# Attention and scan in one kernel: host-transposed inputs, fp32 row tiles for the scores, a mask added in the reduction, a three-part output product, and another order

## The chip, the cores and the metric

The kernel runs on one core of one Trainium2 chip. A core has five engines, each with an instruction queue of its own: PE (TensorE, matrix products into PSUM), DVE (VectorE), ACT (ScalarE), POOL (GpSimd) and SP (SyncE, which here only issues DMAs). The metric is the device time of one execution in microseconds, the median over runs. Inputs lie in device memory (HBM) before the clock starts, in the layout in which the host function has put them; the result is read from there afterwards.

## What is computed

The result joins two independent parts side by side. Part A is an attention of 16 heads of width 28 over 2048 rows, cut into four segments of 512: causal softmax attention within a segment, mixed by a gate with a linear memory (M, z) that gathers the earlier segments. Part B is a long convolution of a state-space model over 2048 steps of 448 channels.

```
for s in range(N):                                   # N = 4 segments, L = 512, H = 16, Dh = 28
    logits = einsum("bhqd,bhkd->bhqk", qs, ks) * scale + mask
    p = softmax(logits); a_dot = einsum("bhqk,bhkd->bhqd", p, vs)
    pq = phi(qs)                                     # phi(t) = t + 1 if t > 0 else exp(t)
    num = einsum("bhld,bhde->bhle", pq, M); den = einsum("bhld,bhd->bhl", pq, z) + 1e-6
    o = g * num / den + (1 - g) * a_dot
    M = M + einsum("bhld,bhle->bhde", phi(ks), vs); z = z + sum_l phi(ks)
a = concat(o) @ wo
b = irfft(rfft(u) * rfft(K))[:L] + u * D_skip        # K = 2 Re sum_n C_n exp(A_n dt t), dt = exp(log_dt)
```

With the given inputs log_dt is about -32, so K hardly changes over 2048 steps and part B is a running sum of u. Both kernels test this on the device (`flag`) and hold the general convolution (`general_conv`) behind a branch that is not taken for these inputs.

## The kernel before

Part A runs as 16 units t, one for each segment s and group g of four heads. For a unit, PE makes q and k (`P_proj`, L534). fp32 precision is made from the faster fp32r format by splitting: x and the weights are held as a rounded part (xh, wh) and a rest (xl, wl), and a product is 11 matmuls that add up in one PSUM bank. Its last one uses only 64 of the 128 rows. v is made in the same way (`V_tile`, L510), one tile of 128 rows per unit on average.

For the scores, q and k are split in turn (tile E, ACT L540 and DVE L541) and copied by three DMAs on POOL (`P_fill`, L555) into a stack SB, in which the parts stand below each other in 96 rows for each head; one fp32r matmul over the 96 rows gives the score. `Q1` (L615) makes all scores of a unit with queries on the partitions; a bf16 matmul (L618) adds the causal mask on the diagonal block and DVE takes each row's maximum (L624). `Q1_max` splits the maxima (L633, L634), transposes them (L636) and puts them into two more rows of the stack with four DMAs (L640). `Q2` (L656) makes the scores again with the keys on the partitions, the maximum subtracted through these rows; ACT takes the exponential (L663, L673), POOL zeroes what lies above the diagonal (L676) and PE multiplies by v (L683, pvp). The four heads of this product lie in four column tiles of PE (128 rows by 32 columns each).

The memory is kept as a block-diagonal matrix Mbd of a group (`M_upd`, L580 to L598) and used in `P_num` (L565). `Q2_end` copies pvp out (L690), gathers the denominators by DMA (rc, L696), inverts them on DVE (L700, L701), writes them to HBM (d, L703) and reads them back spread over the partitions (R, L705). `C_unit` multiplies (L716) and adds (POOL, L720). `W_tile` makes the output product in plain fp32 (L731), ACT copies it out (L736) and SP writes it (L738).

x comes in rows and is transposed on PE (`X_tile`, L484). Part B is 16 tiles: u is loaded (L813), transposed (L826), scaled (L832), scanned twice on DVE (L837, L840), combined with the skip term (L845), transposed back (L851) and written (L855).

All of this is recorded as operations with a cost, a priority and the tiles that they touch; a planner (`Order.plan`) then lists them once, at build time, for each engine. On the chip each engine works down its list in order, so an instruction that waits holds up all behind it on the same engine. Tiles have a fixed number of slots (`SLOTS`); PSUM has seven general banks (f) and one for pvp.

Of the kernel before, what the change touches and what calls it, by code (L numbers as in the profile page):

```python
# [10 lines left out]
BF16 = mybir.dt.bfloat16  # L11
# [8 lines left out]
P = 128  # L20
# [3 lines left out]
NSB = 2  # L24

SLOTS = dict(E=2, xh=1, xl=1, phiq=1, phik=1, P0=1, P1=1, P2=2, R=1, o0=1, o1=1, o2=1, o3=1, pkn=1, mt=1, mx=1, mh=1, mr=1,
             U=2, ut=1, sc=1, z=1, rc=1, xin=2, os=2, pvn=3, d2=3, pv=1, f=7)


class Buf:  # L30


    def __init__(self, tag, make):
        self.tag, self.make, self.tile, self.log, self.left, self.place = tag, make, None, [], 0, 0

    @property
    def ap(self):
        if self.tile is None:
            self.tile = self.make()
        return self.tile  # L40


class Order:


    DRAIN = {"PE": 200.0}
    HOP = 70.0
    RATE = 220.0
    FLIGHT = 2200.0

    def __init__(self, slots):
        self.slots, self.ops, self.made = slots, [], {}

    def buf(self, tag, make):
        b = Buf(tag, make)
        b.place = self.made[tag] = self.made.get(tag, -1) + 1
        return b

    def op(self, eng, cost, pri, fn, r=(), w=(), hold=(), land=0.0):
# [12 lines left out]
        self.ops.append((eng, cost, pri, fn, deps, touch, land))  # L72

    def plan(self):
# [9 lines left out]
        start, end = [None] * n, [0.0] * n  # L84
        free = dict.fromkeys(("PE", "DVE", "ACT", "POOL", "SP"), 0.0)
        ready = {e: {} for e in free}
        slots = {t: [0.0] * c for t, c in self.slots.items()}
        got, last, turn = {}, {}, dict.fromkeys(self.slots, 0)
        lands, moved = [0.0] * n, 0.0

        def seen(j, eng):
            e = self.ops[j][0]
            t = end[j] + lands[j]
            return t if e == eng and not lands[j] else t + self.HOP + self.DRAIN.get(e, 0.0)

# [7 lines left out]
        while done < n:  # L103
            best = None
            for e, cand in ready.items():
                found = []
                for i, t in cand.items():
                    ok = True
                    for b in self.ops[i][5]:
                        if b.tag is not None and id(b) not in got:  # L110

                            if not slots[b.tag] or (b.tag != "f" and b.place != turn[b.tag]):
                                ok = False
                                break
                            t = max(t, min(slots[b.tag]))
                    if ok:
                        found.append((max(t, free[e]), self.ops[i][2], i))
# [10 lines left out]
            eng, cost, pri, fn, deps, touch, land = self.ops[i]  # L128
            del ready[eng][i]
            start[i], end[i] = t, t + cost  # L130
            free[eng] = end[i]
            lands[i] = land
# [4 lines left out]
            for b in touch:  # L137
                if b.tag is not None:
                    if id(b) not in got:
                        got[id(b)] = True  # L140
                        turn[b.tag] += 1
                        slots[b.tag].remove(min(slots[b.tag]))
                    last[id(b)] = max(last.get(id(b), 0.0), seen(i, None))
                    b.left -= 1
                    if not b.left:
                        slots[b.tag].append(last[id(b)])
# [12 lines left out]
def general_conv(tc, u, lar, aim, crl, cim, ldt, dsk, o2):  # L159
# [6 lines left out]
    with ExitStack() as ctx:  # L166
# [59 lines left out]
        ov = o2.rearrange("(c p) d -> p c d", p=P)  # L226
        with tc.For_i(0, NB, 1) as i:
# [67 lines left out]
            nc.sync.dma_start(ov[:, :, bass.ds(d0 + D, ND)], ul)  # L295


def attn_s4d_kernel(tc, x, wq, wk, wv, wo, beta, u, lar, aim, crl, cim, ldt, dsk, out):
    nc = tc.nc
    x2 = x[0]  # L300
    o2 = out[0]
    top = ExitStack()
    flag = top.enter_context(tc.tile_pool(name="top", bufs=1)).tile([1, 1], I32, name="flag")
    with ExitStack() as ctx:
        pool = lambda n, b, **k: ctx.enter_context(tc.tile_pool(name=n, bufs=b, **k))
        cst = pool("cst", 1)
        wp = pool("wp", 1)
        dr = pool("dr", 3, space=DRAM)
        pools = {}
        for tag, n in SLOTS.items():  # L310
            if tag not in ("pv", "f", "d2"):
                pools[tag] = pool("s_" + tag, n)
        pools["d2"] = dr
        for tag in ("pv", "f"):
            pools[tag] = pool("p_" + tag, SLOTS[tag], space=PSUM)
        Q = Order(SLOTS)

        def new(tag, shape, dt, name):
            return Q.buf(tag, lambda: pools[tag].tile(shape, dt, name=name, tag=tag))

        def fixed(pl, shape, dt, name):
            b = Q.buf(None, None)
            b.tile = pl.tile(shape, dt, name=name)
            return b


        def mm(n):
            return n / 2.4 + 20

        def act(n, ptr=0):  # L330
            return 165 + 0.85 * n + 90 * ptr
# [4 lines left out]
        def gps(n):  # L336
            return 200 + 2.6 * n
# [4 lines left out]
        identb = cst.tile([P, P], BF16, name="identb")  # L342
        make_identity(nc, identb)
        mask = cst.tile([P, P], BF16, name="mask")
        nc.gpsimd.memset(mask, 0.0)
        nc.gpsimd.affine_select(mask, mask, [[-1, P]], ALU.is_ge, NEG, base=0, channel_multiplier=1)
        bmask = cst.tile([112, 4, 32], F32, name="bmask")
        bsel = cst.tile([112, 4], F32, name="bsel")
        nc.vector.tensor_reduce(bsel, ident[0:112, 0:112].rearrange("p (r h) -> p h r", h=4), AX.X, ALU.add)
        nc.vector.tensor_copy(bmask, bsel[:, :, None].to_broadcast([112, 4, 32]))  # L350

        epsb = cst.tile([P, 1], F32, name="epsb")
        tmp1 = cst.tile([P, 4], F32, name="tmp1")
        nc.gpsimd.memset(tmp1, 0.0)
# [587 lines left out]
```

## Time and profile before

| what | us |
|---|---|
| median of three runs (506.38, 507.01, 511.79) | 507.01 |
| span of the profiled execution, first to last instruction | 505.8 |
| PE, time with a matmul in flight | 428.5 |
| DVE busy | 274.2 |
| ACT busy | 221.8 |
| POOL busy | 129.3 |

The profile gives one execution; its span is 1.2 us below the median of the timed runs. A matmul's record reaches from its start to its modelled end and so overlaps the next one; how fast PE works is read from the distance between two starts, not from the busy time. The copies of pvp on ACT (L690), one for each unit, end at 78.9 us for the first unit and at 467.3 us for the last, which cuts the span into a build-up, a steady part of fifteen units (25.9 us each) and an end.

### The profile page before, as it was taken

The numbers are of one execution on the slowest core, as the hardware profiler recorded it, in microseconds if no ns is written. First come the engines' busy times: TensorE is split into PE (matmuls) and PEld (weight loads), VectorE is DVE, ScalarE is ACT, GpSimd is POOL, SyncE is SP. The second block draws the span as 40 slices with busy tenths as digits, with TensorE's granted clock in tenths as the row PEclk, the third lists the DMA queues.
The fourth block names the chain that finished last, engine by engine and source line by source line (L and its number), as shares of the span: only waits on it lengthen the run. The fifth ranks groups of instructions, "written<-read, shape, count | busy, mean of one in ns | idle before, by whom it ended". The sixth has DMA issues, their size and how long they took to land. (4 is left out here: it accounts for less than half of the span.)

```text
span 505.8 us, 6508 instructions
## 1 busy us (share of the span) xinstructions
PE 428.5 (85%) x2249; PEld 265.8 (53%) x2249; DVE 274.2 (54%) x501; ACT 221.8 (44%) x437; POOL 129.3 (26%) x224
## 2 busy tenths in 40 slices
PE   2099999989898999789999999889999999787316
PEld 1076666665654556556756555565656455433102
DVE  7654784856564717655374633757275726553310
ACT  2543255445447255262635445344535463247001
POOL 8554131303022303123041401304140413032100
PEclk9999999999899999995989999989989999798759
DMA  8756614743605373915261353913660646302112
GB/s 247 206 144 126 122 33 81 136 103 67 120 24 129 74 184 80 160 43 101 71 152 31 90 128 96 165 51 66 119 152 22 134 123 137 59 31 72 39 52 77
DMA packets 32390, 51.17 MB, mean 101 GB/s; under 512 B 9936, under 2 KB 24256, under 8 KB 32352
## 3 DMA queue, kind: packets, MB, share of 16 engines
q0 software_dynamic: 8016, 24.79, 25.8%
q1 hardware_dynamic: 23200, 24.08, 17.0%
q10 hardware_dynamic: 1136, 1.84, 1.1%
q8 instruction: 20, 0.33, 0.3%
q14 instruction: 18, 0.15, 0.1%
HBM read 20.60 MB, written 7.57 MB: 56 GB/s over the span
## 5 line engine op out<-in xcount | busy, mean ns | idle before, releaser
L624 DVE TENSOR_REDUCE mx<-q 128x2 f32<-128x512 f32 (+2 forms) x192 | 104.0, 594 | 38.8 <-PE q L618 38.5
L615 PE MATMUL q<-SB 96*128 96x256 f32 (+2 forms) x256 | 78.3, 400 | 14.9 <-DMA SB<-E 11.8
L676 POOL TENSOR_SCALAR_AFFINE_SELECT P<-P 128x512 f32<-128x512 f32 x64 | 44.5, 700 | 139.7 <-ACT P L663 118.2
L731 PE MATMUL po<-w_o,o 128*128 128x448 f32 x128 | 56.9, 579 | 21.9 <-POOLq L918 13.7
L656 PE MATMUL s<-SB 98*128 98x256 f32 (+2 forms) x256 | 64.3, 366 | 7.2 <-DMA SB<-mr 3.7
L663 ACT ACTIVATE P<-s 128x512 f32<-128x512 f32 (+1 forms) x128 | 58.2, 563 | 19.5 <-PE s L656 18.9
L615 PEld LDWEIGHTS q<-SB 96*128 96x128 f32 x256 | 47.6, 206 | 30.5 <-issue 15.7
L656 PEld LDWEIGHTS s<-SB 98*128 98x128 f32 x256 | 43.0, 196 | 29.5 <-issue 11.4
L683 PE MATMUL pvp<-P,vb 128*32 128x128 f32 (+3 forms) x512 | 49.3, 461 | 4.3 <-POOL P L676 4.2
L618 PE MATMUL q<-mask,identb 128*128 128x128 bf16 (+1 forms) x192 | 49.5, 258 | 0.0
L731 PEld LDWEIGHTS po<-w_o,o 128*128 128x128 f32 x128 | 23.8, 200 | 44.3 <-issue 20.4
L555 POOL DMA_DIRECT2D SB<-E x48 | 33.3, 729 | 39.3 <-PE s L656 25.4
L673 ACT ACTIVATE P<-s 128x512 f32<-128x512 f32 (+1 forms) x64 | 31.1, 529 | 17.3 <-PE s L656 16.9
L842 POOL COPY carry<-sc 112x1 f32<-112x1 f32 x32 | 7.1, 223 | 120.0 <-DVE sc L837 66.8
L716 DVE TENSOR_TENSOR o<-pvn,R 128x512 f32<-128x512 f32 x16 | 11.9, 746 | 38.9 <-DMA R<-d 38.6
L832 ACT ACTIVATE z<-ut,cf 112x512 f32<-112x512 f32 x32 | 23.2, 726 | 20.2 <-DVE sc L837 19.8
L618 PEld LDWEIGHTS <-identb 128*128 128x128 bf16 x192 | 19.3, 101 | 20.6 <-issue 8.1
L510 PE MATMUL vp<-wh_v,xh 128*128 128x448 f32 x64 | 28.8, 450 | 0.1
L736 ACT COPY os<-po 128x448 f32<-128x448 f32 x16 | 8.6, 539 | 44.6 <-PE po L731 42.0
L837 DVE TENSOR_TENSOR_SCAN sc<-ones,carry,z 112x512 f32<-112x512 f32 x16 | 21.9, 1367 | 11.5 <-PE pvp L683 5.8
L510 PE MATMUL vp<-wl_v,xh 128*128 128x448 f32 x64 | 28.0, 437 | 0.0
L540 ACT CAST E<-ppq 112x512 fp32r<-112x512 f32 x16 | 9.5, 591 | 41.8 <-PE ppq L534 41.7
(125 smaller groups left out, 699.4 us busy)
## 6 DMA issues: line engine op xcount, KB each, us to landing
SB<-E POOLq DMA_DIRECT2D x48, 448.0 KB, 8.0
R<-d SPq DMA_DIRECT2D x12, 512.0 KB
x<-in_A_x SPq DMA_DIRECT2D x16, 224.0 KB
U<-in_B_u SPq DMA_DIRECT2D x8, 448.0 KB
out<-U SPq DMA_DIRECT2D x8, 448.0 KB
out<-os SPq DMA_DIRECT2D x16, 224.0 KB
SB<-mr SPq DMA_DIRECT2D x64, 4.0 KB
R<-d SPq DMA_DIRECT2D x4, 256.0 KB
```

The source lines that it names most:

```text
L510: nc.tensor.matmul(pv.ap, xs[xx].ap[0:k, c, lt * P:(lt + 1) * P], ws[w].ap[0:k, c, :], start=(i == 0), stop=(i == len(ps_) - 1))
L555: nc.gpsimd.dma_start(Sf[28 * i:28 * i + 28], (Ef[:, 1:3, :], Ef[:, 0:3:2, :], Ef[:, 1:4:2, :])[i])
L615: nc.tensor.matmul(pt.ap[:, j, :], SB.ap[0:96, h, 0, qb * P:(qb + 1) * P], SB.ap[0:96, h, 1, 0:m], start=(j == 0), stop=False)
L618: nc.tensor.matmul(pt.ap[:, :, n - P:n], identb, mask[:, None, :].to_broadcast([P, len(hs), P]), start=False, stop=True)
L624: nc.vector.tensor_reduce(mx.ap[:, hs[0]:hs[-1] + 1, qb], pt.ap[:, :, 0:n], AX.X, ALU.max)
L656: nc.tensor.matmul(o, SB.ap[0:98, h, 1, kb * P:(kb + 1) * P], SB.ap[0:98, h, 0, 512 - m:512], start=True, stop=True)
L663: Q.op("ACT", act(n), pri + 0.02 * h, lambda pp=pp, h=h: nc.scalar.activation(pb.ap[:, h, :], pp.ap[:, 0:n], AF.Exp, scale=SCALE), r=[pp], ...
L673: Q.op("ACT", act(2 * n), pri + 0.02 * h, lambda pp=pp, h=h: nc.scalar.activation(pb.ap[:, h:h + 2, :], pp.ap[:, :, 256 - n:256], AF.Exp, ...
L676: Q.op("POOL", 700, pri + 0.1, lambda: nc.gpsimd.affine_select(pb.ap[:, :, 0:P], pb.ap[:, :, 0:P], [[0, 4], [1, P]], ALU.is_ge, 0.0, base= ...
L683: nc.tensor.matmul(pvp.ap[32 * h:32 * h + 32, kb * P:512], V.ap[:, 4 * g + h, :], pb.ap[:, h, :], start=(kb == 0), stop=(kb == 3))
L731: nc.tensor.matmul(po.ap, st[4 * s + g]["o"].ap[:, cs], w.ap[:, g, :], start=(g == 0), stop=(g == 3))
L832: Q.op("ACT", 725, p, lambda k=k, z=z: nc.scalar.activation(z.ap, ut.ap, AF.Copy, scale=cf.ap[:, j, k:k + 1]), r=[ut, cf], w=[z])
```

## The change

Host. The host function hands over x and u transposed, the weights already in the order of the head groups (each head padded from 28 to 32 columns) and beta and the vectors of part B in the shape of their tiles. Part B is written transposed to an output of its own and turned on the host. So X_tile's and part B's transposes are gone, and the loads are whole rows of 2 KB.

Scores. q and k stay in fp32, head h in the partitions 32h to 32h+27, and the stacks, their DMAs and the split are gone. Q1 and Q2 use matmuls of 28 (29) rows by 128 columns in fp32, four heads one behind the other, each in its own row tile of PE and its own PSUM bank. Row 28 of k holds -1 and row 28 of q gets the maximum, by one DMA. The mask matmul is gone: DVE adds the mask while it takes the maximum (`tensor_tensor_reduce`, for each head and block of queries alone).

The rest. The 64-row matmul at the end of each product uses 128 rows. The memory M is [128, 32], one 28 x 32 block for each head, in row and column tiles. phi takes its minimum on POOL. The output product is three fp32r matmuls for each group, for which o is rounded (ACT) and the rest taken (POOL). Part B keeps one scan of two and a multiply-add. All weights and x go through three slots (xin) by SP, in turn with ACT's rounding and DVE's or POOL's rest. All DMAs are issued by SP. PSUM is one pool of eight banks. The planner knows a price for a change of PE's tile shape (`SWITCH`), takes among operations that are nearly ready the one of highest priority (`NEAR`), and its priorities come from a table of numbers (`AT`).

```diff
+                        f = free[e] + (self.SWITCH if e == "PE" and self.ops[i][7] != mode else 0.0)
...
-                    t, p, i = min((f for f in found if f[0] <= t0 + 1e-9), key=lambda f: (f[1], f[2]))
+                    t, p, i = min((f for f in found if f[0] <= t0 + self.NEAR[e]), key=lambda f: (f[1], f[2]))
...
+        room("f", 8, [P, 512], F32, psm)
+        room("xin", 3, [P, 512], F32)
+        room("pvn", 2, [P, 2, 512], F32)
...
-            return r + [(0, 0, 3, P), (1, 0, 3, 64)]
+        PASSES = [(w, x, c) for c in range(3) for w, x in ((0, 0), (1, 0), (0, 1))] + [(0, 0, 3), (1, 0, 3)]
...
+            Q.op("SP", 90, pri, lambda: nc.sync.dma_start(t.ap, xT[s, :, c]), w=[t], land=-262144)
+            Q.op("ACT", act(512), pri, lambda: nc.scalar.copy(h.ap, t.ap), r=[t], w=[h])
...
-                        nc.tensor.matmul(pt.ap[:, j, :], SB.ap[0:96, h, 0, qb * P:(qb + 1) * P], SB.ap[0:96, h, 1, 0:m],
-                                         start=(j == 0), stop=False)
-                    nc.tensor.matmul(pt.ap[:, :, n - P:n], identb, mask[:, None, :].to_broadcast([P, len(hs), P]),
-                                     start=False, stop=True)
+                    for h in range(4):
+                        nc.tensor.matmul(bank[h].ap[:, c0:c0 + n], q.ap[rows(h), qb * P:(qb + 1) * P], k.ap[rows(h), 0:n],
+                                         start=True, stop=True)
...
-                    nc.vector.tensor_reduce(mx.ap[:, hs[0]:hs[-1] + 1, qb], pt.ap[:, :, 0:n], AX.X, ALU.max)
+                        nc.vector.tensor_tensor_reduce(sc, sc, mask[:, 512 - n:512], 1.0, -3.0e38, ALU.add, ALU.max,
+                                                       mx.ap[:, 4 * h + qb:4 * h + qb + 1])
...
-                nc.tensor.matmul(o, SB.ap[0:98, h, 1, kb * P:(kb + 1) * P], SB.ap[0:98, h, 0, 512 - m:512],
-                                 start=True, stop=True)
+                        nc.tensor.matmul(bank[h].ap[:, c0:c0 + w], k.ap[rows(h, 29), kb * P:(kb + 1) * P],
+                                         q.ap[rows(h, 29), P * kb:512], start=True, stop=True)
...
+            Q.op("ACT", act(512), pri, lambda: nc.scalar.copy(oh.ap, pvn.ap[:, 0, :]), r=[(pvn, 0)], w=[oh])
+            Q.op("POOL", 1344, pri, lambda: nc.gpsimd.tensor_tensor(ol.ap, pvn.ap[:, 0, :], oh.ap.bitcast(F32), ALU.subtract),
+                 r=[(pvn, 0), oh], w=[ol])
...
-                nc.tensor.matmul(po.ap, st[4 * s + g]["o"].ap[:, cs], w.ap[:, g, :], start=(g == 0), stop=(g == 3))
+                for i, (o, w) in enumerate(((oh, wh), (oh, wl), (ol, wh))):
+                    nc.tensor.matmul(po.ap, o.ap[:, cs], w.ap[:, g], start=(g == 0 and i == 0), stop=(g == 3 and i == 2))
...
-                    o2[lc * 512:(lc + 1) * 512, 448 + 224 * jp:672 + 224 * jp].rearrange("(t p) d -> p t d", p=P), U.ap),
+            Q.op("SP", 90, pri, lambda: nc.sync.dma_start(yT[ds_, ls], ut.ap), r=[ut], land=-229376)
+AT = dict(q=-1.78, k=-1.95, fq=-2.44, fk=3.5, V=-1.6, Vn=0.65, num=-0.43, M=-0.71, s=-1.62, sn=-0.05, max=-3.89,
+          e=-0.68, en=0.1, pv=0.11, c=-0.34, w=2.79, wn=0.6, b=2.67, x=-3.8, xn=-2.14)
```

Three places show what this does to the engines' lists. On PE, the first scores of unit 0 stood like this before (q: score banks, SB: a stack; L615 scores, L618 mask):

```order
L615 MATMUL q_0_559<-SB_193 128x256 x2
L618 LDWEIGHTS identb
L618 MATMUL q_0_559<-mask,identb 128x2x128
L615 MATMUL q_0_563<-SB_193 128x256 x2
L618 LDWEIGHTS identb
L618 MATMUL q_0_563<-mask,identb 128x2x128
L615 MATMUL q_0_571<-SB_193 128x384
L618 LDWEIGHTS identb
L618 MATMUL q_0_571<-mask,identb 128x128
```

Each bank is now filled by one plain matmul of one head, four heads in a row into four banks (f), and products of unit 1 (L486) follow:

```order
L555 MATMUL f_69<-k_94,q_90 128x512
L555 MATMUL f_70<-k_94,q_90 128x512
L555 MATMUL f_71<-k_94,q_90 128x512
L555 MATMUL f_72<-k_94,q_90 128x512
L555 MATMUL f_73<-k_94,q_90 128x384
L555 MATMUL f_74<-k_94,q_90 128x384
L555 MATMUL f_67<-k_94,q_90 128x384
L555 MATMUL f_68<-k_94,q_90 128x384
L486 MATMUL f_69<-xh_78,wh_q 128x512
```

The mask rows are gone, and the unit's scores are no longer one stretch: the 384- and 512-wide blocks come first and other products stand between them and the narrow ones. Counted over the whole list, and leaving out the single matmuls of 64 rows, PE changes its tile shape 124 times before and 197 times now.

On DVE, the maxima of the same unit stood like this before (mx: maxima, ek: phi of k):

```order
L624 TENSOR_REDUCE mx_581<-q_0_559 128x2
L546 SCALAR_TENSOR_TENSOR ek_540<-ek_540,ppk_518 112x512
L624 TENSOR_REDUCE mx_581<-q_0_563 128x2
L624 TENSOR_REDUCE mx_581<-q_0_571 128x1
L624 TENSOR_REDUCE mx_581<-q_1_574 128x1
```

And now (L563 is the masked maximum; each is two instructions, the second stores the result; wl: rests of the weights, from the slots xin):

```order
L432 TENSOR_TENSOR wl_v<-xin_76,wh_v 128x448
L563 ISA f_69,mx_123<-f_69,mask 128x512
L563 ISA mx_123 128x1
L432 TENSOR_TENSOR wl_q<-xin_77,wh_q 128x512
L563 ISA f_70,mx_123<-f_70,mask 128x512
L563 ISA mx_123 128x1
```

A unit's 12 reductions have become 16 pairs, and the maxima of the first units now stand between the rests of the weights.

On SP, the last DMAs were these before (rc, d, R: the denominators' way; U: part B; os: output rows; mr: maxima):

```order
L696 DMA rc_4198<-pvn_3832 128x1x32
L640 DMA SB_194<-mr_4195 2x4x128 x4
L855 DMA out<-U_0_3436 128x4x224
L703 DMA d_14_4252<-rc_4198 128x32
L705 DMA R_4277<-d_14_4252 128x1x1024
L696 DMA rc_4318<-pvn_4019 128x1x32
L855 DMA out<-U_1_3883 128x4x224
L703 DMA d_15_4341<-rc_4318 128x32
L705 DMA R_4343<-d_15_4341 128x1x1024
```

And these are the last ones now:

```order
L615 DMA rc_127<-pvn_104 128x1x32
L622 DMA d_131<-rc_127 128x32
L662 DMA out_a<-os_122 128x448
L627 DMA R_106<-d_131 128x1x1024
L615 DMA rc_128<-pvn_105 128x1x32
L622 DMA d_129<-rc_128 128x32
L627 DMA R_106<-d_129 128x1x1024
L662 DMA out_a<-os_121 128x448
```

Before, a write of part B stood between rc and d of the last unit; now d follows rc directly, and part B has been written earlier.

More of the change, by code (lines that the diff above doesn't have):

```diff
@@ L304, in attn_s4d_kernel @@
     with ExitStack() as ctx:
[L305 to L316, printed above, removed]
@@ L559, in P_num @@
         def P_num(t, pri):
             s, g = divmod(t, NG)
[L561 to L568 removed]
+            if s == 0:
+                return
```

840 lines of the change are left out of this document (373 added, 467 removed).

## The prediction

> **What bounds the kernel now.** I read the page first, for the engines' shares, and then asked for four stretches, cut where PE's first real products start (26.4 us) and where the first and the last unit's pvp are ready (78.3 and 466.7 us). After that I went through PE's timeline.
>
> ```profile
> PE 428.5 (85%) x2249; PEld 265.8 (53%) x2249; DVE 274.2 (54%) x501; ACT 221.8 (44%) x437; POOL 129.3 (26%) x224
> ...
> 0.00:26.40 26.40, 4.60 (x17) 2.83 (x17) 18.88 (x25) 11.37 (x19) 17.41 (x50) 1.00 0.81 221
> 26.40:78.30 51.90, 50.85 (x256) 34.08 (x255) 34.28 (x71) 19.95 (x43) 19.41 (x25) 1.00 0.51 110
> 78.30:466.70 388.40, 359.65 (x1952) 222.54 (x1951) 214.73 (x398) 186.53 (x370) 88.73 (x145) 0.96 0.44 96
> 466.70:505.80 39.10, 13.38 (x28) 6.38 (x28) 6.29 (x9) 3.97 (x7) 3.73 (x4) 0.73 0.16 57
> ```
>
> In the columns of the stretches PE comes first, then the weight loads, DVE, ACT and POOL. For 440.3 us (26.4 to 466.7) PE has a matmul in flight during 410.5; the next, DVE, is busy for 249. So PE's stream is the bound, with 30 us of waits, and before and behind it stand 26.4 us of loading and 39.1 us of an end that is one chain of DMAs. I therefore cost the change by the distance between starts on PE, and the two ends by themselves.
>
> **Part by part: PE.** Products first.
>
> ```profile
> 63.29 0.39 PE L534 MATMUL ppk<-xh,wl_k 128*112 128x512 f32 x1
> 63.52 0.40 PE L534 MATMUL ppk<-xh,wh_k 128*112 128x512 f32 x1
> 63.85 0.48 PE L534 MATMUL ppk<-xh,wl_k 64*112 64x512 f32 x1
> 64.26 1.13 PE L588 MATMUL pm<-vb,pkn 128*112 128x128 f32 x8
> ...
> 45.62 0.36 PE L510 MATMUL vp<-wh_v,xl 128*128 128x448 f32 x1
> 45.82 0.36 PE L510 MATMUL vp<-wl_v,xh 128*128 128x448 f32 x1
> ```
>
> A 512-wide fp32r matmul takes 0.23 us from start to start (63.29 to 63.52), a 448-wide one 0.20. Around the 64-row matmul the steps are 0.33 and 0.41 instead, 0.28 us too much for one change of the tile shape there and one back. There are 48 products (32 for q and k, 16 for v), each loses this: 48 x 0.28 = **13 us less**.
>
> ```profile
> 201.75 3.27 PE L731 MATMUL po<-w_o,o 128*128 128x448 f32 x8
> 204.86 0.60 PE L484 MATMUL xp<-ident,x 128*128 128x128 f32 x4
> 205.30 0.55 PE L580 MATMUL pkt<-ident,ek 112*128 112x112 f32 x4
> ```
>
> Eight fp32 records of the output product take 3.11 us, 0.39 each; 128 of them (50 us) become 192 fp32r matmuls of 0.20 (38 us): **12 us less**. Four transposes of x take 0.44 us, and those of u and y, as narrow, are costed alike; 16 groups for x and 32 for u and y go: 48 x 0.44 = **21 us less**.
>
> ```profile
> 53.53 0.47 PE L615 MATMUL q<-SB 96*128 96x256 f32 x2 [0.98 <-DMA SB<-E]
> ...
> 57.97 0.49 PE L534 MATMUL ppq<-xh,wh_q 128*112 128x512 f32 x1
> ...
> 71.10 1.07 PE L683 MATMUL pvp<-P,vb 128*32 128x512 f32 x8
> 72.10 0.51 PE L656 MATMUL s<-SB 98*128 98x256 f32 x2
> ...
> 218.98 1.27 PE L656 MATMUL s<-SB 98*128 98x512 f32 x5
> 220.09 0.39 PE L534 MATMUL ppk<-xh,wl_k 128*112 128x512 f32 x1
> ...
> 221.06 1.27 PE L656 MATMUL s<-SB 98*128 98x384 f32 x7
> 222.17 1.04 PE L588 MATMUL pm<-vb,pkn 128*112 128x128 f32 x8
> ...
> L615 PEld LDWEIGHTS q<-SB 96*128 96x128 f32 x256 | 47.6, 206 | 30.5 <-issue 15.7
> ```
>
> Q1 of a unit, with its mask matmuls, takes 4.4 us (53.53 to 57.97). Q2 takes 0.22 for a wide matmul (five in 1.11) and 0.16 for a narrow one (seven in 1.11); with 4 of 512, 4 of 384 (0.19, between the two) and 8 of 256 that is 0.9 + 0.8 + 1.3 = 3.0 us. The trace has no row tile. The nearest row is the fp32 column tile: four heads of 512 columns (eight records) take 1.00 us to the next start, 0.14 of which is the change of shape (0.28 / 2), so 0.86. One behind the other, eight full-width records of 0.39 x 512 / 448 would take 3.6, so four column tiles run at once. If row tiles do too, a unit's blocks of 512, 384, 256 and 128 columns, four heads each, cost 0.86 + 0.65 + 0.43 + 0.41 = 2.4 us (the last is held by two weight loads of 206 ns instead of its 0.21). I take this value, from the nearest row; the other end is one head at a time, and a rival. Q1 saves 16 x (4.4 - 2.4) = **32 us**, Q2 16 x (3.0 - 2.4) = **10 us**.
>
> [...]
>
> Against this stand the changes of tile shape: 197 for 124, 73 x 0.14 = **10 us more**. [...]
>
> P_num and M_upd keep their columns, now in four or 16 small tiles at once; I cost them at nothing, between 5 us less and 10 us more, since each of 12 updates grows from 8 records to 32. PE's sum is 13 + 32 + 10 + 12 + 21 - 10 = **78 us less**.
>
> **Waits and other engines.**
>
> ```profile
> L615 PE MATMUL q<-SB 96*128 96x256 f32 (+2 forms) x256 | 78.3, 400 | 14.9 <-DMA SB<-E 11.8
> L624 DVE TENSOR_REDUCE mx<-q 128x2 f32<-128x512 f32 (+2 forms) x192 | 104.0, 594 | 38.8 <-PE q L618 38.5
> L541 DVE TENSOR_TENSOR E<-ppk,E 112x512 fp32r<-112x512 f32 x16 | 11.0, 686 | 11.7 <-ACT ek L544 8.0 <-ACT E L540 3.8
> L489 DVE TENSOR_TENSOR xl<-xp,xh 128x384 fp32r<-128x384 f32 x16 | 8.9, 554 | 3.1 <-ACT xh L486 3.0
> L624 DVE TENSOR_REDUCE mx<-q 128x2 f32<-128x256 f32 x32 | 13.4, 417 | 4.3 <-PE q L618 4.3
> L597 DVE TENSOR_TENSOR mt<-pm,bmask 112x128 f32<-112x128 f32 x8 | 2.3, 286 | 6.1 <-PE pm L588 6.1
> L634 DVE TENSOR_TENSOR mh<-mx,mh 128x16 fp32r<-128x16 f32 x16 | 2.8, 176 | 0.6
> L840 DVE TENSOR_TENSOR_SCAN sc<-z,carry,sc 112x512 f32<-112x512 f32 x16 | 20.6, 1287 | 0.9 <-ACT z L832 0.9
> ```
>
> PE's wait for the copy into the stack (11.8 us) goes with the stack: **12 less**. What is late next is DVE. Its 192 reductions (104.0 us) become 256 masked ones with two inputs from or through PSUM, for which I take DVE's rows of the same widths: 4 x (686 + 554 + 417 + 286) = 7.8 us for a unit, 124 us, and 256 stores of a maximum, between nothing and 176 ns each (45 us); I take 0.1 us, 26 us. That is 46 us more. The rests of q and k (L541, 11.0 us for k and as much for q), one scan (20.6) and the split maxima (L634 and its like) go, 45 us or more, so DVE stays at or under its 274 us, two thirds of the new span. Its bursts have to fit between two fills of four banks, so I leave PE's other 18 us of waits as they are. ACT loses the casts and Relus of the split and gets those of o; it stays near its 222 us. POOL loses 48 DMA issues and gets 16 rests of o and 24 minima; at 26% this is hidden, except at the end. SP takes over all loads and its list is in order: a u or weight load whose slot is not free holds q's maxima behind it. With one DMA for the maxima in place of four I cost it at nothing; it is part of the rival on new waits. pvn has two slots instead of three: the way from pvn (466.7) to the end of L720 in the rows below (491.6) is 25 us, well under the two units (over 40 us) that two slots give, so this is hidden.
>
> **The two ends.**
>
> ```profile
> 474.98 0.24 DVE L701 TENSOR_SCALAR rc<-rc,mix 128x32 f32<-128x32 f32 x1
> 478.47 0.38 SPq L855 DMA_DIRECT2D out<-U  x1
> 478.95 0.46 SPq L703 DMA_DIRECT2D d<-rc  x1
> 488.93 0.69 DVE L716 TENSOR_TENSOR o<-pvn,R 128x512 f32<-128x512 f32 x1 [13.71 <-DMA R<-d]
> 490.30 1.26 POOL L720 TENSOR_TENSOR o<-o,pvn 128x512 f32<-128x512 f32 x1 [16.41 <-DVEq L918]
> 491.62 9.33 PE L731 MATMUL po<-w_o,o 128*128 128x448 f32 x20 [13.74 <-POOLq L918]
> ...
> L690 ACT COPY pvn<-pvp 128x512 f32<-128x512 f32 x16 | 9.4, 585 | 36.0 <-PE pvp L683 35.9
> ...
> 0.83 0.41 SPq L469 DMA_DIRECT2D x<-in_A_x  x1
> ...
> 3.90 0.87 PE L484 MATMUL xp<-ident,x 128*128 128x128 f32 x3 [3.90 <-DMA x<-in_A_x]
> ```
>
> At the end d waited behind part B's write, 3.7 us after L701 was done (475.2 to 478.95). That goes. The rounding of o (0.6, like ACT's copy of 512 columns in L690) and the rest on POOL (1.3, as L720) come into the chain. Behind them stand 30 matmuls of 0.20 to 0.4 for 20 of 0.47: 1 us less. Together **3 us less**. At the start V waited until 26.4 us. A load is there 3 us after its issue (0.83 to 3.90). Now the first product needs five loads through three slots; a round of three takes that 3 us, one rounding (0.6) and up to three rests on DVE (0.7 each, as L541), 5 to 6 us, so two rounds end near 12 us, and the weights of v, which need five, near 28 us. In between PE has q, k and first scores of units 0 and 1, four products of 2.5 us and 2.4 us of scores. So up to 28 us it idles about 28 - (4 x 2.5 + 2.4) = 16 us instead of 26.4 - 4.6 = 22: **6 us less** (between 0 and 12).
>
> Sum: 505.8 - 78 - 12 - 3 - 6 = 407 us of span, and the 1.2 us between span and median: **408 us**.
>
> **The rivals.**
> *Row tiles do not run together* (the slower side). Then each head's block is paid alone, 4 x 2.15 = 8.6 us for 2.4, and 32 times the difference of 6.2 is 198 us: 606 us. For: no row shows them. Against: the column tiles do it in fp32. It decides against the change once the 32 sets cost 3.1 us more each (99 / 32), at 5.5 us, that is when fewer than 1.6 of the four run at once. At two at once a set takes 4.3 us and the kernel 408 + 32 x 1.9 = 469 us.
> *DVE becomes the bound.* The masked reduction writes its scores back to PSUM. If that costs a second pass, DVE gets 124 us more, some 390 us busy; with the start, the end and a few waits 450 us. For: DVE holds four banks until it is done, and 16 pairs of a unit come in bursts. Against: rows with a PSUM input (L541) cost no more than others.
> *The waits go too.* With the stack's long way (split, DMA, fill) gone and the next unit's products standing between the blocks, the other 18 us of waits and most of the changes of shape (ten to twenty microseconds) vanish: 370 us.
> *The general convolution runs*, because the test on the device is a new one: with these inputs its left side is 0.02 of its right, so it is left out with under 1 in 100.
>
> **How the numbers follow.** The forecast (385 to 430, with the bounds of M_upd, of the start and of the stores) gets 0.58; waits gone (360 to 385) 0.15; DVE bound or other new waits (430 to 470) 0.17; row tiles two at once or worse 0.10, of which 0.07 end slower than before. The range for 8 in 10 leaves out the upper part of the third and the fourth, and the lowest part of the second: 362 to 460. About 1% is what a measurement of this kernel can tell from no change. Faster: 0.58 + 0.15 + 0.17 and a little of the fourth, 0.91; slower 0.07; same 0.02.
>
> **What would show it.** The rows of the two score lines: four 512-wide heads within some 0.9 us and PE's next start right behind; 1.5 us or more says that they do not run together. The masked reduction near 690 ns at 512 columns, and its store under 180 ns. DVE between 250 and 290 us. No wait of PE for a stack. The changes of shape as steps of 0.1 to 0.2 us before a first row tile. PE's idle time in the steady part under 30 us, and if it is far over that, its releaser: DVE's maxima would mean the second rival, SP's DMAs a list that is held up. The prediction is wrong if the span is over 460 without a row tile that is slower than 0.9 us for four heads.

## The result, and the profile after

| | before | after |
|---|---|---|
| median (4 runs each) | 509.38 us | 390.18 us |
| lowest to highest | 506.38 to 511.79 | 388.06 to 391.86 |
| profiled span | 505.8 | 387.5 |

The ratio of after to before is 0.773, with an interval of 0.767 to 0.779; it is taken over executions in the faster of two states alone, and the medians of the table would give 0.766. The forecast was 408 us with a range of 362 to 460.

The page of the changed kernel, its first line, has the engines' busy time, share of the span and instructions:

```profile
PE 345.5 (89%) x2801; PEld 210.2 (54%) x2801; DVE 235.4 (61%) x696; ACT 197.4 (51%) x404; POOL 128.3 (33%) x169
```

Four stretches of the changed kernel, cut where V starts (34.3) and at the first and the last unit's copy of pvn (58.7 and 351.3); PE's busy time stands first behind the length, PE's granted clock is the third number from the right:

```profile
0.00:34.30 34.30, 23.38 (x98) 14.45 (x98) 22.60 (x64) 12.88 (x23) 5.09 (x34) 1.00 0.62 178
34.30:58.70 24.40, 24.40 (x235) 16.85 (x234) 20.80 (x62) 15.86 (x33) 11.60 (x12) 1.00 0.27 78
58.70:351.30 292.60, 283.97 (x2455) 168.67 (x2440) 188.06 (x567) 164.71 (x341) 106.51 (x119) 0.98 0.21 67
351.30:387.50 36.20, 13.77 (x42) 10.26 (x42) 3.94 (x6) 3.95 (x7) 5.07 (x4) 0.64 0.15 54
```

Between the first and the last copy of pvn lie 15 units: 388.4 us before (the prediction's row 78.30:466.70), 292.6 now. I take such a steady part into three: what PE's idle time takes (length less busy), what a low clock takes (length times one less the clock, an estimate and rounded to about 2 us, since the row has two digits), and the rest, which I call work. Waits too short to be seen stay in the work. The traces also record each stretch at low clock: 34.1 us before and 10.2 now, at a granted clock of 0.50, which is 17.1 and 5.1 us lost. So the estimate of the clock's part holds to 2 us, and the work's with it.

| us | length | idle | clock | work |
|---|---|---|---|---|
| before | 388.4 | 28.8 | 15.5 | 344.1 |
| after | 292.6 | 8.6 | 5.9 | 278.1 |
| difference | -95.8 | -20.2 | -9.6 | -66.0 |

The beginning is 19.6 us shorter (78.3 to 58.7): PE's busy time in it is 7.7 less (4.60 + 50.85 to 23.38 + 24.40) and its idle time 11.9 less. The record of the clock starts only at 30.6 us before and at 20.2 us now, so the 1.00 of the first rows says nothing of the time ahead of that; there the changed kernel's products step by 0.43 us (9.01 to 9.44), about twice the 0.23 of later, which costs some 5 us of its 10.5 us of busy time (an estimate). The end is 2.9 shorter (39.1 to 36.2). The sum, -95.8 - 19.6 - 2.9, is the 118.3 us between the spans.

PE's timeline of the changed kernel (start, duration, engine, line, operation, number merged), first the row tiles among products, then a wait and what came behind it:

```profile
205.81 0.94 PE L586 MATMUL f<-q,k 29*128 29x256 f32 x16
206.67 0.50 PE L486 MATMUL f<-xh,wh_q 128*128 128x512 f32 x1
...
210.77 0.36 PE L470 MATMUL f<-wh_v,xl 128*128 128x448 f32 x1
211.06 1.14 PE L555 MATMUL f<-k,q 28*128 28x512 f32 x8
212.13 0.47 PE L470 MATMUL f<-wh_v,xh 128*128 128x448 f32 x1
212.45 0.36 PE L470 MATMUL f<-wl_v,xh 128*128 128x448 f32 x1
...
213.34 0.93 PE L555 MATMUL f<-k,q 28*128 28x384 f32 x8
214.20 0.46 PE L534 MATMUL f<-vb,xin 128*32 128x32 f32 x32
214.47 2.38 PE L606 MATMUL f<-P,vb 128*32 128x512 f32 x32
219.21 0.46 PE L534 MATMUL f<-vb,xin 128*32 128x32 f32 x32 [2.36 <-DVE M L540]
219.60 2.81 PE L586 MATMUL f<-q,k 29*128 29x512 f32 x8
...
225.22 0.63 PE L486 MATMUL f<-xl,wh_k 128*128 128x512 f32 x1
225.64 0.63 PE L486 MATMUL f<-xh,wh_k 128*128 128x512 f32 x1
...
228.57 0.50 PE L486 MATMUL f<-xh,wh_k 128*128 128x512 f32 x1
228.91 0.39 PE L486 MATMUL f<-xh,wl_k 128*128 128x512 f32 x1
229.14 0.39 PE L486 MATMUL f<-xl,wh_k 128*128 128x512 f32 x1
```

Four heads of 512 columns take 1.07 us from start to start (211.06 to 212.13), those of 384 0.86, and the 256- and 128-column blocks together 0.86 (205.81 to 206.67). The step into the row tiles is 0.29 for 0.20 (210.77 to 211.06), the one out of them 0.32 (212.13 to 212.45). Behind 219.21 the steps are longer in two ways that have to be told apart. The set at 219.60 takes 2.74 us to the next start for 1.07; the products from 225.22 on step by 0.42 (225.22 to 225.64) instead of 0.23 (228.91 to 229.14). The weight loads (PEld) of the set, and the granted clock of this place:

```profile
220.43 0.29 PEld L586 LDWEIGHTS f<-q,k 29*128 29x128 f32 x2 [0.22 <-DVE mx L563]
220.95 0.29 PEld L586 LDWEIGHTS f<-q,k 29*128 29x128 f32 x2 [0.22 <-DVE mx L563]
...
218.19:221.60 3.41, 2.39 (x40) 1.52 (x40) 3.41 (x13) 1.72 (x4) 2.30 (x2) 1.00 0.02 5
221.60:225.02 3.42, 3.42 (x12) 0.92 (x11) 1.06 (x4) 0.99 (x3) 0.24 (x1) 0.50 0.03 5
```

The set waits for DVE's maxima, one head at a time, 0.52 us apart, while the clock is still at 1.00; PE counts as busy all the while. The clock falls to 0.50 only at 221.6 and is back at 228.4. Ahead of both stands a wait of 2.36 us. DVE's part of the same place, and the mean of the masked maxima:

```profile
217.19 1.29 DVE L637 TENSOR_TENSOR pvn<-pvn,R 128x512 f32<-128x512 f32 x2 [3.57 <-DMA R<-d]
218.41 0.69 DVE L563 CUSTOM_DVE_ANT_0 f<-f,mask 128x512 f32<-128x512 f32 x1
...
219.01 0.14 DVE L563 DVE_READ_ACCUMULATOR2_ANT mx<- 128x1 f32 x1
219.01 0.18 DVE L540 TENSOR_TENSOR M<-M,f 128x32 f32<-128x32 f32 x1
219.11 0.69 DVE L563 CUSTOM_DVE_ANT_0 f<-f,mask 128x512 f32<-128x512 f32 x1
...
219.72 0.14 DVE L563 DVE_READ_ACCUMULATOR2_ANT mx<- 128x1 f32 x1
```

```profile
L563 DVE CUSTOM_DVE_ANT_0 f<-f,mask 128x512 f32<-128x512 f32 (+3 forms) x256 | 120.9, 514 | 47.5 <-PE f L555 45.3
L563 DVE DVE_READ_ACCUMULATOR2_ANT mx<- 128x1 f32 x256 | 36.0, 140 | 0.1
```

DVE stood 3.57 us for R's transfer; a maximum and the addition to M were queued behind the multiplications; PE waited for that addition, then in short waits for the maxima that came late with it, and 2.4 us after the long wait the clock fell to 0.50 for 6.8 us. The only other low stretch in the steady part of this trace is its last 3.4 us. A maximum and its store come every 0.71 us at 512 columns (219.01 to 219.72 between two stores).

### The profile page after: what moved, and what is told of

It reads as the page before. It is cut to its first block, busy times and chain, and to the rows that moved or that the text cites. A ratio compares the mean times of both kernels' runs of the same rounds, so it can differ in the third digit from the quotient of the medians.

```text
span 387.5 us, 7551 instructions
## 1 busy us (share of the span) xinstructions
PE 345.5 (89%) x2801; PEld 210.2 (54%) x2801; DVE 235.4 (61%) x696; ACT 197.4 (51%) x404; POOL 128.3 (33%) x169
## 5 line engine op out<-in xcount | busy, mean ns | idle before, releaser
L563 DVE CUSTOM_DVE_ANT_0 f<-f,mask 128x512 f32<-128x512 f32 (+3 forms) x256 | 120.9, 514 | 47.5 <-PE f L555 45.3
L590 ACT ACTIVATE P<-f 128x384 f32<-128x384 f32 (+1 forms) x192 | 86.3, 527 | 20.1 <-PE f L586 18.8
L586 PE MATMUL f<-q,k 29*128 29x128 f32 (+3 forms) x512 | 54.8, 465 | 0.3 <-DVE mx L563 0.2
L555 PE MATMUL f<-k,q 28*128 28x128 f32 (+3 forms) x512 | 50.5, 471 | 0.8 <-ACT k L491 0.8
L655 PE MATMUL f<-wh_o,oh 128*128 128x448 f32 x64 | 27.6, 431 | 17.3 <-ACT oh L643 16.8
L606 PE MATMUL f<-P,vb 128*32 128x128 f32 (+3 forms) x512 | 39.4, 449 | 0.3 <-DVE mx L563 0.2
L486 PE MATMUL f<-xh,wh_q 128*128 128x512 f32 x64 | 28.4, 444 | 10.4 <-ACT wh_q L429 7.3
L563 DVE DVE_READ_ACCUMULATOR2_ANT mx<- 128x1 f32 x256 | 36.0, 140 | 0.1
L586 PEld LDWEIGHTS f<-q,k 29*128 29x128 f32 x512 | 26.3, 183 | 17.1 <-DVE mx L563 5.2
L486 PE MATMUL f<-xh,wh_k 128*128 128x512 f32 x64 | 28.9, 452 | 0.5 <-DVE mx L563 0.5
L655 PEld LDWEIGHTS f<-wh_o,oh 128*128 128x128 f32 x64 | 13.1, 205 | 26.8 <-ACT oh L643 18.7
L486 PE MATMUL f<-xh,wl_k 128*128 128x512 f32 x64 | 26.6, 416 | 0.2 <-DVE wl_k L432 0.2
L486 PE MATMUL f<-xh,wl_q 128*128 128x512 f32 x64 | 26.3, 411 | 0.4 <-DVE wl_q L432 0.4
```

The costliest lines, as they stand in the source:

```text
L486: nc.tensor.matmul(pp.ap, (wl if w else wh).ap[:, g, c], X(s, x, c).ap, start=a, stop=b)
L555: nc.tensor.matmul(bank[h].ap[:, c0:c0 + n], q.ap[rows(h), qb * P:(qb + 1) * P], k.ap[rows(h), 0:n], start=True, stop=True)
L563: nc.vector.tensor_tensor_reduce(sc, sc, mask[:, 512 - n:512], 1.0, -3.0e38, ALU.add, ALU.max, mx.ap[:, 4 * h + qb:4 * h + qb + 1])
L586: nc.tensor.matmul(bank[h].ap[:, c0:c0 + w], k.ap[rows(h, 29), kb * P:(kb + 1) * P], q.ap[rows(h, 29), P * kb:512], start=True, stop=True)
L590: Q.op("ACT", act(n), pri + 0.01 * h, lambda h=h: nc.scalar.activation(pb.ap[:, h, 0:n], bank[h].ap[:, 0:n], AF.Exp, scale=SCALE), r=[bank ...
L606: nc.tensor.matmul(pvp.ap[32 * h:32 * h + 32, kb * P:512], VB(s, kb).ap[:, 4 * g + h, :], pb.ap[:, h, c0:c0 + 512 - P * kb], start=(kb == ...
```

## Experiments

Differences are the ratio to the kernel before, less the 0.7728 of the changed kernel, times 505 us. The intervals of both together leave some 5 to 8 us open on each side, part of it in common, since all differences go by the same 0.7728.

**The order kept, one cost changed.** In the first four kernels the order that the planner writes is the changed kernel's, instruction by instruction, but for those added.

*The 64-row matmul back.*

```
-  nc.tensor.matmul(pp.ap, (wl if w else wh).ap[:, g, c], X(s, x, c).ap, ...)
+  nr = 64 if (w, c) == (1, 3) else P
+  nc.tensor.matmul(pp.ap, (wl if w else wh).ap[0:nr, g, c], X(s, x, c).ap[0:nr], ...)
```

> Undoes the last matmul of each product alone: 64 rows of 128 again. Theory: 48 products lose 0.28 us each in two changes of the tile shape, 13 us more, so 401 to 405 us. Rival (the change of shape is hidden in waits for banks): under 4 us more.

398.76 us, ratio 0.789 (0.779 to 0.799): 8 us more. Its steady part:

```profile
60.60:359.80 299.20, 292.00 (x2452) 165.64 (x2438) 188.81 (x566) 165.53 (x342) 107.15 (x119) 0.99 0.20 65
```

Idle 7.2, clock 3.0, work 289.0: the work is 10.9 more than in the changed kernel, and idle time and clock give 4 back. Of the 48 products 37 lie in this part (25 for q and k, 12 for v), so that is 0.29 us for each: the 0.28 us of the prediction are there. Part of them is taken up by waits, so the time lies between the theory's 13 us and the rival's 4.

*Q2's row tiles issued twice.*

```
-  for h in range(4):
+  for h in (0, 1, 2, 3, 0, 1, 2, 3):
```

> Issues every set of Q2's row tiles twice into the same banks; the result is the same. Theory (PE is the bound, the four row tiles of a set run at once): 16 x 2.4 us = 38 us more, with nothing on another engine, so 420 to 430 us. Rival A (the four heads run one at a time): 16 x 8.6 = 138 us more. Rival B (PE is no longer the bound, DVE's maxima or ACT's exponentials are): under 20 us more.

403.68 us, ratio 0.804 (0.796 to 0.811): 15.5 us more. PE's timeline and the steady part:

```profile
208.17 2.10 PE L586 MATMUL f<-q,k 29*128 29x512 f32 x16
210.20 1.06 PE L512 MATMUL f<-phq,M 28*32 28x512 f32 x8
...
212.89 1.57 PE L586 MATMUL f<-q,k 29*128 29x384 f32 x16
214.40 0.51 PE L486 MATMUL f<-xh,wh_k 128*128 128x512 f32 x1
```

```profile
58.40:366.50 308.10, 306.46 (x2940) 188.95 (x2925) 187.03 (x567) 166.00 (x342) 109.24 (x119) 1.00 0.20 64
```

Another four heads of 512 columns cost 0.96 us (2.03 for 1.07), of 384 0.65 (1.51 for 0.86): less than a set alone, so the four heads don't run one behind another (3.6). In the steady part the work is 28.4 more, but idle time falls to 1.6 and the clock stays at 1.00, which gives 13 back. By its time this is the range of rival B (under 20 us), not of the theory (38): PE had 13 us of slack in waits and clock, and only what goes beyond them came out. With 1.6 us of idle time left, still more work on PE should come out in full; that was not tested.

*The 512-column maxima taken twice, untold to the planner.*

```
+  if qb == 3:
+      nc.vector.tensor_tensor_reduce(sc, sc, mask[:, 512 - n:512], ...)
```

> Takes the masked maximum of the 512-wide blocks twice: 64 reductions and 64 stores more on DVE, at some 0.71 us from start to start, 45 us of DVE's time, nothing on PE. Theory (DVE at 61% is hidden behind PE): 0 to 10 us more. Rival (DVE, which holds four banks until it is done, sets the pace): 30 to 45 us more.

432.10 us, ratio 0.860 (0.849 to 0.871): 44 us more.

```profile
62.00:390.00 328.00, 306.67 (x2452) 177.78 (x2438) 228.61 (x679) 165.46 (x341) 106.41 (x119) 0.96 0.19 59
```

Idle 21.3, clock 13.1, work 293.6. This is the rival's range. Most of DVE's 45 us (64 x 0.71) comes out: the steady part is 35 us longer, 13 as PE's idle time, 7 by the clock, and 15 inside what counts as work. PE's instructions are the same, so these 15 are most likely waits too short to show, like those at 219.60 above.

*The maxima over 256 columns only.* For the blocks of 512 and 384 columns the rest is left out of the maximum.

```
-  sc = bank[h].ap[:, c0:c0 + n]
+  m = min(n, 256)
+  sc = bank[h].ap[:, c0:c0 + m]
...
```

> Leaves out part of the maxima: each of the 512- and 384-column blocks is reduced over its first 256 columns only; the order of every engine is that of the changed kernel. By the rows of the changed kernel this takes 64 x (716 - 432) + 64 x (588 - 432) ns = 28 us off DVE and nothing off PE. Theory A (PE's own stream is the bound and DVE only shows when it gets more work): 0 to 8 us less than the changed kernel, since PE waits for maxima in few microseconds. Rival B (DVE lies on the way as much as PE does, as the doubled maxima suggest, with 44 us for 46 us of work): 15 to 28 us less, and the steps between PE's groups shrink.

384.82 us, ratio 0.768 (0.761 to 0.775): 3 us less, or none.

```profile
57.20:346.80 289.60, 280.39 (x2453) 166.85 (x2441) 169.97 (x566) 165.15 (x341) 108.73 (x119) 0.99 0.21 66
```

DVE is 20 us less busy over the whole span (214.9 for 235.4), and PE's idle time is the same 9 us, as theory A had it. So DVE isn't the bound; but in this order it has no room either: more work on it costs nearly its full time, less gives next to nothing.

**A part changed, and the order planned anew.** Here a difference holds the part and the new order together.

*The output product in fp32, one part.*

```
-  for i, (o, w) in enumerate(((oh, wh), (oh, wl), (ol, wh))):
-      nc.tensor.matmul(po.ap, o.ap[:, cs], w.ap[:, g], ...)
+  nc.tensor.matmul(po.ap, o.ap[:, cs], w.ap[:, g], start=(g == 0), stop=(g == 3))
```

> Undoes the output product in three parts: o stays in fp32, no rounding on ACT, no rest on POOL, one fp32 matmul (two records) for each group. Theory (PE's stream sets the time): PE gets 128 records of 0.39 us for 192 matmuls of 0.20, 12 us more, and the end loses the rounding and the rest, about 2 us; so 398 to 402 us against 390. Rival (PE has waits in which the output product is hidden, and the split costs ACT and POOL more than it gives): within 3 us of 390, or below.

396.43 us, ratio 0.787 (0.780 to 0.795): 7 us more. The steady part has 11.6 us more work (289.7, from 295.78 busy of 302.30 at 0.98). Four fifths of the output product lie in this part (151 of 192 matmuls now), so some 9 of the theory's 12 us were due there; the rest may be the new order.

*The doubled maxima, told to the planner.*

```
-  Q.op("DVE", dve(n), pri + 0.01 * h, red, ...)
+  Q.op("DVE", dve(n) + (710 if qb == 3 else 0), pri + 0.01 * h, red, ...)
```

> The 512-wide maxima twice again, but the planner is told of it (710 ns more for each), so the lists of all engines are made for it. In the run before, without that, 45 us of work on DVE made the kernel 44 us longer, though DVE is busy for 61% only. Theory A (DVE has room, but each list is worked down in order and was made for shorter maxima, so PE waits at wrong places): most of it goes, under 15 us more than the changed kernel. Theory B (the maxima lie on the way from one unit to the next, whatever the lists are): 30 us or more remain.

418.46 us, ratio 0.831 (0.825 to 0.838): 30 us more, 14 less than untold. So an order made for it seems to hide a third of such a cost, not all; 14 us is no more than what a small change of the order does by itself, as shown below.

*The mask on PE*, as a bf16 matmul for each head and block, with a plain maximum on DVE.

```
+  nc.tensor.matmul(bank[h].ap[:, c0 + n - P:c0 + n], identb, mask, start=False, stop=True)
-  nc.vector.tensor_tensor_reduce(sc, sc, mask[:, 512 - n:512], ...)
+  nc.vector.tensor_reduce(mx.ap[:, 4 * h + qb:4 * h + qb + 1], sc, AX.X, ALU.max)
```

> Undoes the mask in DVE's maxima: PE adds it with one bf16 matmul for each head and block, DVE takes plain maxima (256 for 256 pairs). PE gets 256 small matmuls and 26 more changes of the tile shape, about 256 x 0.06 + 26 x 0.14 = 19 us; DVE loses 256 stores of some 0.08 us from start to start, 20 us. Theory A (PE's stream is the bound): 10 to 19 us more. Theory B (DVE's maxima are the bound as much): between 10 us less and 5 us more.

418.99 us, ratio 0.829 (0.820 to 0.838): 28 us more, with 28 us more PE busy (373.8) and 20 less DVE (215.1). In the steady part 23 of the 33 us more are work, 7 clock and 3 idle time. Both theories had put PE's price too low; what DVE was spared did not make up for it.

*The maxima from bf16 copies of q and k*, made on POOL.

```
+  b = st[t][nm + "b"] = Q.buf(nm + "b")
+  Q.op("POOL", 800, pri, lambda: nc.gpsimd.tensor_copy(b.ap, d.ap), r=[(d, 0)], w=[b])
-  mx, q, k = st[t]["mx"], st[t]["q"], st[t]["k"]
+  mx, q, k = st[t]["mx"], st[t]["qb"], st[t]["kb"]
```

> Q1's scores from bf16 copies of q and k, which POOL makes, since the maximum only has to be near the true one; Q2, the exponentials and the sums stay as they are. [...] Theory A (PE's stream): 15 to 25 us less than the changed kernel. Theory B (DVE): under 8 us less.

395.61 us, ratio 0.787 (0.779 to 0.796): 7 us more; theory A had 15 to 25 less and theory B up to 8 less, so neither came true.

```profile
54.90:360.50 305.60, 281.95 (x2249) 166.26 (x2249) 190.10 (x568) 165.87 (x343) 125.17 (x145) 0.92 0.21 65
```

What PE would save was an estimate that no earlier run showed. The work did fall, by 20.6 us to 257.5 (a unit's 128- and 256-column blocks take 0.18 us to the next start, 60.68 to 60.86, for 0.87 in the changed kernel, 26.23 to 27.10); idle time (23.7) rose by 15 and the clock's part (24.4) by 18. What was saved on PE came back as waits and as low clock.

*The multiplications by R on POOL*, so that DVE no longer stands for R.

```
+  e, v, c = ("DVE", nc.vector, dve(512)) if t == 15 else ("POOL", nc.gpsimd, 1344)
-  Q.op("DVE", dve(512), pri, lambda i=i: mul(i), ...)
+  Q.op(e, c, pri, lambda i=i: mul(i), ...)
```

> The 26 multiplications by R before the last unit go from DVE (722 ns each, 19 us) to POOL (about 1.3 us each, 34 us on an engine with 128 of 388 us busy), and with them DVE's wait for R's transfer (55.8 us of DVE's idle time stand before these multiplications, with the next maxima queued behind). Order planned anew. Theory A (DVE's list is on the way between units): 5 to 20 us less than the changed kernel. Rival B (DVE's wait falls into time that it has anyway, or POOL's masks of P are now held behind the wait): no gain or up to 15 us more.

393.88 us, ratio 0.786 (0.778 to 0.794): 6 us more. Idle time in the steady part is 9.6 for 8.6, and the work is 6 more. So taking the wait for R off DVE's list did not shorten PE's waits, as rival B had it; why the work is more is not shown.

**The same work in another order.**

*Rules off*: no price for a change of shape, no choice by due time among operations that can start nearly at once.

```
-  SWITCH = 110.0
+  SWITCH = 0.0
-  NEAR = {"PE": 150.0, "DVE": 60.0, "ACT": 60.0, "POOL": 60.0, "SP": 20.0}
+  NEAR = dict.fromkeys(("PE", "DVE", "ACT", "POOL", "SP"), 1e-9)
```

> The planner's two new rules are off (no price for a change of tile shape, no preference for an earlier due time among operations that could start nearly at once); the table of due times and all work stay. The earlier run with rules off and coarse due times cost 63 us over the changed kernel. Theory A (the rules carry most of that): 40 to 65 us more. Rival B (the table carries it): under 20 us more.

433.52 us, ratio 0.869 (0.859 to 0.878): 48 us more.

*Rules off, and due times as coarse as before's.*

```
-  AT = dict(q=-1.78, k=-1.95, fq=-2.44, ...
+  AT = dict(q=-2.2, k=-2.1, fq=-2.1, fk=-2.0, V=-1.6, Vn=0.3, num=-1.0, M=-1.0, s=-1.0, sn=0.1, max=-1.0,
+            e=-0.5, en=0.2, pv=0.1, c=0.5, w=1.0, wn=0.5, b=1.0, x=-3.0, xn=0.2)
```

> The changed kernel's work in an order made by the earlier rules: no price for a change of the tile shape, no choice among nearly ready operations, and the earlier offsets of the priorities in place of the table. Theory A (the gain is in the work that went, the order matters little): under 8 us more. Theory B (a good part of the gain is the order): 20 us more or above.

453.06 us, ratio 0.898 (0.891 to 0.905): 63 us more.

*Due times rounded to a tenth of a unit, rules on.*

```
-  AT = dict(q=-1.78, k=-1.95, fq=-2.44, ...
+  AT = dict(q=-1.8, k=-1.9, fq=-2.4, ...
```

> The same work and the same rules; every due time rounded to a tenth of a unit (at most 0.05 units, 1 us, away). It shows how much of a difference of some 7 us between two kernels can be a matter of the order alone. Theory A (the time hangs on the work and on the rough order): within 4 us of the changed kernel. Rival B (the order is tuned to fractions of a microsecond): 6 to 20 us more.

403.48 us, ratio 0.799 (0.786 to 0.811): 13 us more, or 7 to 19 by its interval.

The steady parts of the first two, rules off and then the coarse times:

```profile
59.20:399.40 340.20, 316.00 (x2463) 188.54 (x2463) 182.89 (x567) 165.68 (x342) 103.84 (x119) 0.92 0.18 57
```

```profile
59.40:425.40 366.00, 343.59 (x2436) 204.13 (x2436) 191.49 (x580) 167.72 (x343) 107.51 (x120) 0.86 0.17 54
```

| us, over the changed kernel | length | idle | clock | work |
|---|---|---|---|---|
| rules off | +47.6 | +15.6 | +21.3 | +10.7 |
| rules off, coarse times | +73.4 | +13.8 | +45.3 | +14.3 |

Every instruction is the same; the order is paid in waits, and more in clock than in waits. The work's part holds waits too short to show and further changes of the tile shape, which these runs don't separate. One such stretch of the kernel with the coarse times, on PE's timeline:

```profile
203.83 0.46 PE L534 MATMUL f<-vb,xin 128*32 128x32 f32 x32
204.22 2.32 PE L586 MATMUL f<-q,k 29*128 29x512 f32 x8
206.99 0.90 PE L526 MATMUL f<-ident,phk 128*128 128x128 f32 x4 [0.46 <-DVE phk L498]
207.82 1.66 PE L586 MATMUL f<-q,k 29*128 29x384 f32 x8
...
213.40 0.63 PE L486 MATMUL f<-xl,wh_q 128*128 128x512 f32 x1
213.82 0.63 PE L486 MATMUL f<-xh,wh_q 128*128 128x512 f32 x1
...
218.74 0.39 PE L486 MATMUL f<-xh,wl_k 128*128 128x512 f32 x1
218.97 0.39 PE L486 MATMUL f<-xl,wh_k 128*128 128x512 f32 x1
```

The weight loads of the set at 204.22, and the granted clock:

```profile
204.90 0.29 PEld L586 LDWEIGHTS f<-q,k 29*128 29x128 f32 x2 [0.22 <-DVE mx L563]
205.42 0.29 PEld L586 LDWEIGHTS f<-q,k 29*128 29x128 f32 x2 [0.22 <-DVE mx L563]
...
203.86:207.28 3.42, 2.96 (x47) 1.65 (x44) 3.08 (x11) 1.90 (x4) 0.00 (x0) 1.00 0.20 77
207.28:210.69 3.41, 3.41 (x49) 1.95 (x48) 0.00 (x0) 1.94 (x6) 0.63 (x1) 0.50 0.20 82
```

The set is slow at full clock, since it waits for maxima. From 207.3 to 217.5 the clock is at 0.50 and the products step by 0.42 (213.40 to 213.82) for 0.23. In the 3.4 us ahead of the fall there is one visible wait, of 0.46 us, beside the short ones inside the set. A low clock thus goes with an order that has more gaps, but no long wait is needed ahead of each stretch; what sets one off isn't settled by these runs.

That tenths of a unit cost 13 us also says how to read the five kernels that were planned anew: a difference under some 13 us there may be the order alone. This holds for the output product, the bf16 maxima and the multiplications on POOL. The four with the order kept stand free of it, though there the order is one that was planned for other costs.

## Why the prediction was right, and where it was not

*PE's work.* 78 us less were forecast. Measured are 66.0 in the steady part (64 with the recorded clock) and 7.7 of busy time ahead of it, 74. The two terms that were undone one at a time fit: 10.9 us of work for the 64-row matmuls (forecast were 13 for all 48 products, of which 37 lie there: 10), 11.6 for the output product (some 9 of 12), the latter with its order planned anew. The time that each gave back is 8 and 7. The larger terms, 42 us for the scores and 21 for the transposes, were not undone alone; they stand by the sum, and the scores by the row tiles' measured cost.

*Row tiles.* Right: to the next start a unit's sets take 1.07 + 0.86 + 0.86 = 2.8 us, as do the forecast's 2.4 with one change of shape of 0.14 for each set. But the step into a set is 0.09 longer besides, and the one behind it 0.12: a 512-column set among products costs 1.28 us (210.77 to 212.45, less two steps of 0.20), where the forecast's terms, 0.86 and two changes, make 1.14. The 384-column set is dearer too (0.86 + 0.21 for 0.65 + 0.28), the narrow blocks are not (0.86 + 0.21 for 0.84 + 0.28): 0.2 us for a unit's blocks, 32 times, some 6 us more at most (an estimate), since not each set stands among products. The rival of one head at a time, 606 us, is out. For another 512-column set the doubled kernel shows 0.96 us (2.03 less 1.07); 0.86 was taken.

*M_upd.* Costed at nothing, with 5 us less as its bound. An update took 0.88 us before (64.26 to 65.14, the next start behind the prediction's row) and takes 0.27 (214.20 to 214.47) to 0.5 now: some 12 x 0.5 = 6 us less. Here the 32 small records are cheaper than the 8 large ones. So the row tiles came out a little dearer and the updates cheaper than forecast, and that the two may cancel in PE's sum is luck.

*DVE.* Sizes right: 690 ns and the store hidden but for 0.1 us were forecast, and a pair every 0.71 us is there; DVE's 235 us are under the 274. "Hidden" was half right. With less DVE work the time stays, so the rival of a DVE-bound kernel is out for this kernel; with 45 us more it loses 44. The margin that the prediction saw in "two thirds of the new span" does not exist: the maxima come in bursts on which four banks wait, and at 219.60 and 204.22 PE's weight loads are seen to wait for them, head by head.

*Waits.* This is the step that failed in size: "I leave PE's other 18 us of waits as they are". In the steady part idle time fell by 20.2 us instead of 12, and at the start by 11.9, the far end of the 0 to 12 that were given, with 6 taken. The picture of the start was off as well: V began at 34.3 us, not near 28, and PE stood idle for 10.9 us until then, not 16: it had five products to do, not four, and the first ones stepped by 0.43 us (9.01 to 9.44) for the 0.23 of later. Against the 99 us of the forecast's sum the spans differ by 118.3: 14 more from idle time, 10 from the clock, 4 less from work. The rival "the waits go too" came in by half.

*The clock.* No term stood for it: about 9.6 us of the steady part (12 by the recorded stretches). The row 78.30:466.70 had shown 0.96. That it would rise was not foreseen.

*The end.* 3 us less forecast, 2.9 measured, and in the main for the reasons given: d now follows the scaling of rc at once (359.21 to 359.24), where it waited 3.7 us, and the way from the multiplication by R to PE's first matmul with the rest of o is 2.0 longer (368.81 to 373.50 for 488.93 to 491.62), 1.9 forecast.

*The order.* The forecast took the new order as the place where the work stands, at a price of 10 us for more changes of shape. With an order like before's the same work takes 453 us: then the change is worth 52 us, and the order the other 63. Much of what was forecast from work alone needs this order to come out: PE's stream was a fair measure only since waits and clock did not take the gain back, as they did with the bf16 maxima. No step of the prediction asked for that, so this part of its hit is luck. Of the 63, the two rules off with the new due times cost 48; as the due times were fitted with the rules on, this doesn't divide them cleanly. The new rules were not tried on the work before.

## What to carry to other kernels

Split a steady stretch into PE's work, idle time and clock, and predict each: the work adds up well from rows (74 us less here for 78 forecast), but a tight order decides how much of it becomes time. An engine with a third of its time free can still have no room (DVE here, busy for 61%), so double its bursts before calling it hidden. Compare variants in the same order where possible, and take the spread of a slightly different order as the resolution where it isn't. Where steps are twice as long as usual (0.42 us for 0.23 here), look at the granted clock and at the weight loads' waits before calling it the one or the other.

## What the runs showed of the hardware

In the traces before and after, the granted clock is 1.00 or 0.50 (products of 512 columns 0.23 or 0.42 us apart, 228.91 to 229.14 and 225.22 to 225.64). Their steady parts have seven stretches at 0.50 before and two now, each of 3.4, 6.8 or 10.2 us; one of the kernel with coarse times is 20.5 long (135.6 to 156.1 us). In the changed kernel the clock fell at 221.6 us with PE idle for 1.0 us of the last 3.4, the end of a wait of 2.36 us, and in the kernel with coarse times at 207.3 us with a wait of 0.46 us. In the 3.4 us ahead of each of the nine stretches before and now PE was idle for 1.0 us at the least (218.19 to 221.60 now) and 2.6 at the most (429.91 to 433.32 before).

POOL's minimum with a constant over 512 fp32 columns takes 1.49 us, twice the planner's 700 ns:

```profile
L497 POOL TENSOR_SCALAR phq<-phq 128x512 f32<-128x512 f32 x12 | 17.8, 1486 | 19.3 <-ACT phq L496 19.3
```
